# Five staging buffers for the query exponentials, and a new order of all steps

## The chip, the cores and the metric

The kernel runs on one core of a Trainium2 chip. The metric is the device time of one execution in microseconds (us). A core has a matrix engine (TensorE, in the profile PE, with its weight loads as PEld), a vector engine (VectorE, DVE), an activation engine (ScalarE, ACT), a general engine (GpSimd, POOL) and a sync engine (SP) that here only issues transfers. Each engine works off its own list of instructions in order. Transfers (DMAs) are issued by SP and ACT and run on 16 shared DMA engines.

## What is computed

```python
# x: 2048 tokens, D = 448; H = 16 heads of Dh = 28; F = 1792; all bf16
xn = layernorm(x)
q, k, v = split(xn @ wqkv)
phi(t) = concat(softmax(t @ w_phi), softmax(-(t @ w_phi)))     # per head, over 28 features
kv = phi(k)^T @ v ;  z = sum over tokens of phi(k)
a = ((phi(q) @ kv) / (phi(q) . z + 1e-6)) @ wo
h = xn @ w1 + b1 ;  b = (h * tanh(softplus(h))) @ w2           # Mish
out = x + a + b
```

Softmax of the queries needs no sum of its own, since numerator and denominator are divided by each other: for the queries only the exponentials of t and of -t are formed, and the two halves are brought together at the end.

## The kernel before

The 2048 tokens are 16 tiles of 128 (t = 0 to 15), taken as eight pairs (u = 0 to 7). 448 rows of a contraction are three chunks of 128 and one of 64; so that half an array never idles, most products are issued as two streams of 64 rows, one for each tile of a pair, and a product of a pair (a *part step* such as `k3`) is split into two halves, `k31` with 8 and `k32` with 6 matmuls. All of them are recorded on line 438.

Everything is unrolled, and the order of all engines comes from one string, `ORDER`: a list of names of steps. `run_order` calls them one after another; each appends its operations to the lists of its engines, with the resources that it reads and writes, and `Program` derives the waits from them. So the order of the names sets the order on every engine and on SP's and ACT's transfer queues, and it also decides which of the eight banks of the matrix engine's accumulators a step gets (`take1`, `take2`: the least recently used bank or pair that nobody holds).

The names: `l...` loads (`lx3` etc. rows of x, `lkm`, `lvm`, `lkt` the weights of k and v, `lqT` those of q transposed, `l1m`, `l1t` W1, `l2` W2, `lo` Wo; a last letter s is SP, a is ACT). `st` are the statistics of a tile (suffix d on DVE, L467 and L468; suffix a on ACT as a Copy with a sum, a small multiplication and a Square with a sum, L459 to L463); `rs` its reciprocal deviation (suffix p on POOL, a or t on ACT), `xn` the normalised pair (suffix d or p), `xt` its transposition: suffix m by a DMA on SP (L521), a or d by seven matmuls on PE (L509) that ACT or DVE copies out. `wtk` and `wmk`, `wmq` fold w_phi into the weights of k and q (L556, L571). `z` are matmuls on constants before the data arrive (L376). `v`, `k`, `q` are the token products of a pair; when the second half is done, `v` is copied out by ACT or DVE, and `k` and `q` get two exponentials on ACT (exk, L600; exq, L661). `kn` normalises the keys: a sum and a reciprocal on DVE (L608, L610), then a multiplication on POOL (`phik`, L612). `kv` adds up phi(k)^T v over all pairs in one bank (L629), `kvz` masks it on DVE and transposes it by a DMA. `e` is the transposition of a tile of query exponentials to EqT by a DMA on SP (L669). `nd` is numerator and denominator of a tile (PE L703, then DVE), `ot` the transposition of its result by a DMA, `wo` and `G` are the output products (L821 and L805 where whole arrays are used), `f` the first product of the feed-forward layer (`f0` the first 1024 tokens, `f1` the last; 14 chunks of F each, in two halves), followed by Mish on ACT (L680). `sto` and `stt` store a pair or a tile.

Space is shared. The tile `actT` has one row of 2048 columns for each of the 14 chunks of F. Rows 6 to 13 hold the exponentials of the keys (E) until `kv` has read them. The exponentials of the queries (Eq) are staged before their transposition in three buffers: a tile of their own, Eq0 (which early on also holds the transposed weights WT), and rows 4 and 5 of `actT`, in turn by pair number. `p_pads` (`pp`) clears the unused columns of a buffer on POOL. So the Mish of a chunk that lies in such a row waits until the transpositions of that buffer have landed, and an exponential waits for the transpositions of the pair that used its buffer before:

```python
w=[("act", fc, q)] + ([("E", fc - FE, s) for s in range(2)] if fc >= FE else
   [x for i in range(3) if EQ_ROWS[i] == fc for x in (("Eq", i, 0), ("Eq", i, 1), ("Eqp", i))])
```

Of the kernel before, what the change touches and what calls it, by code (L numbers as in the profile page):

```python
# [144 lines left out]


ORDER = """
lpa pp2 lx3s pm z12 st6d pi lkms table st7d pw lx1a lkts lba lvma bd rs3t wtk2a xn3d lx2s lqT2 wtk0d st3d pv wtk1a wmk2a
xt3a wtk3d lqT1 wmk0a wmk1a st2d wmk3a st5d v31d rs1p lqT0 st4d xn1d rs2p lqT3 b1 qd lx6s v32a k31 lx0s wmq1a lx4s pp1
wmq0a xn2p l1ts xt1d st14d st15d wmq2a wmq3a k32 k11 st12d rs7p st9d q11 xt2m st8d k12 st10d xn7d q31 rs4p v11d pp0 q12  # L150
xn4p st11d v12d q21 rs5p st13d q32 q22 xn5p k21 st0d l1m2s l1m0s rs6p xt7m v21d k22 st1d v22a ep e3 rs0p v71a pk xt4m
k71 v72a kn3.1 xn6d k72 xt5m k41 xn0d kn3.0 e2 xt6m xt0m v41d e5 k42 l1m1s v42d e4 q41 v51d q42 e6 e8 v52a kn2.0 k61
v61d k62 kn4.0 k01 k51 kn7.0 kn4.1 k02 v62d q51 k52 q52 kn0.0 e7 q61 e9 v01d q62 e12 kn1.1 kn6.1 e10 f0.11 e11 kn1.0
v02d f0.12 kn0.1 f1.01 f0.21 f1.02 f1.21 kn7.1 f1.31 f1.22 los kn2.1 q71 f1.32 f1.51 kn5.0 f0.22 e13 f1.52 q01 q72 q02
f0.61 l2s kn6.0 kv3 kv1 e15 kv2 kn5.1 kv4 kv6 e14 kv7 kv0 kv5 kvz f0.62 f0.71 f0.91 f1.81 f0.72 e1 f1.82 f0.121 f1.111
f0.122 f0.81 f0.92 f1.112 f0.82 f1.91 f0.131 f1.92 e0 nd2 f0.132 f0.31 f0.101 f0.32 nd0 f0.111 f0.102 f0.112 nd1 f1.71
f1.61 f1.72 f0.51 nd3 f1.62 f0.52 f1.41 f1.11 f0.01 f1.12 f0.41 f1.42 ot0m nd5 f0.42 f0.02 wo01 f1.131 f1.101 ot1m nd6
f1.132 G01 nd4 f1.102 G11 ot2m wob nd7 ot3m G02 wo02 f1.121 nd12 G12 f1.122 wo11 nd11 wo22 G31 wo31 nd10 wo12 G21 nd13
ot5m ot6m wo21 wo32 G62 nd8 G22 wo52 G32 nd9 ot4m wo61 G51 nd15 G61 nd14 wo51 G41 wo62 sto6 sto1 wo41 G52 ot7m g14 sto5
wo7F sto2 G42 wo7H sto0 wo42 g15 stt14 sto3 sto4 stt15  # L160
"""


# [5 lines left out]
def _kernel(es, nc, A_x, A_wqkv, A_w_phi, A_wo, B_w1, B_b1, B_w2, out):  # L169
    def sb(name, shape, dtype):  # L170
        return es.enter_context(nc.sbuf_tensor(name, shape, dtype))
# [30 lines left out]
    actT = sb("actT", [P, FC, S], BF16)  # L202
# [7 lines left out]
    EqT = sb("EqT", [P, NT, 2 * G, P], BF16)  # L210
    Eq0 = sb("Eq0", [P, 4 * TCW], BF16)
# [38 lines left out]
    def bank(b, n=1):  # L250
        return PS[:, b * TCW:(b + n) * TCW]
# [177 lines left out]
    def pair_part(key, part, works, r, then):  # L429
        if part == "1":  # L430
            open_[key] = take2()
        b = open_[key]

        def f(e):
            todo = works(b)
            for par, k, c in halves(part, 3, True):
                o, _, lhs, rhs = todo[par]
                ins = e.matmul(o, lhs(c, k), rhs(c, k), start=part == "1" and c == 0, stop=part == "2" and c == 2)  # L438
# [218 lines left out]

    def q_mm(u, part):
        def then(b):
            for s in range(2):  # L660
                op("ACT", lambda e, s=s: e.activation(  # L661
                    Eq_of(u)[:, :, s, :].rearrange("p i (h n) -> p i h n", n=64)[:, :, :, 0:QP],
                    two(b, D).rearrange("p i (h n) -> p i h n", n=QP), ACT.Exp, scale=1.0 if s == 0 else -1.0),
                   r=[pb(b), pb(b + 1), ("Eqp", u % 3)], w=[("Eq", u % 3, s)], tag=f"exq{u}.{s}")
        pair_part(f"q{u}", part, tok_works(u, Wp[0]), [("xnT", u), ("xnU", u)] + [("Wp", 0, c) for c in range(4)], then)

    def q_turn(t):
        u = t // 2
        dma("SP", lambda e: e.dma_start_transpose(EqT[:, t, :, :], Eq_of(u)[:, t % 2, :, :].rearrange("p s c -> p (s c)")),  # L669
            r=[("Eq", u % 3, 0), ("Eq", u % 3, 1)], w=[("EqT", t)], tag=f"eT{t}")  # L670
# [7 lines left out]
    def ffn1(q, fc, part):  # L678
        def then(b):
            op("ACT", lambda e: e.activation(actT[:, fc, q * 1024:(q + 1) * 1024], bank(b, 2), ACT.Mish,  # L680
                                             bias=b1T[:, fc:fc + 1]),
               r=[("b1T",), pb(b), pb(b + 1)],
               w=[("act", fc, q)] + ([("E", fc - FE, s) for s in range(2)] if fc >= FE else
                                     [x for i in range(3) if EQ_ROWS[i] == fc for x in (("Eq", i, 0), ("Eq", i, 1), ("Eqp", i))]), tag=f"mish{q}_{fc}")
# [181 lines left out]
    def add(name, fn, *args):  # L866
        steps[name] = lambda: fn(*args)
# [120 lines left out]
```

## Time and profile before

| what | value |
|---|---|
| median of three runs | 150.57 us (150.38 to 150.88) |
| the profiled execution's own time | 150.35 us |
| its span in the trace | 148.3 us |
| PE busy | 143.7 us (97%) |
| DVE, ACT, POOL busy | 100.7, 72.0, 44.4 us |
| first product that needs data, end of the last matmul | 5.94, about 145.9 us |

The span runs from the first to the last instruction; the profiled execution's own time is some 2 us longer. The share of a busy engine is an average over stages. In a line of the timeline the first number is the start, the second the time until the last of the grouped instructions ends, and x8 their count; a bracket names an idle time before them and what ended it. In the list of waits the numbers are the total in us, how often, and the longest. A matmul's record is longer than the time it takes from the engine, since matmuls are pipelined; what one costs is read from the distance of the starts.

### The profile page before, as it was taken

The page shows a single profiled execution, that of the slowest core. Times are in us where ns is not written, and L with a number is a line of the kernel's source. Part 1 is how long each engine was busy: PE and PEld are TensorE (multiplying, and loading weights), DVE is VectorE, ACT ScalarE, POOL GpSimd, SP SyncE. Part 2 cuts the span into 40 slices and gives each one's busy share as a digit, 9 for nine tenths or more (in the row PEclk, how much of TensorE's full clock was granted, in tenths as well). Part 3 has the DMA queues.
Part 4 walks back from the last instruction along what each step waited for, and adds up shares of the span by engine and source line. Part 5 has one row for each costly group of instructions (what it writes and reads, how often), then busy time and mean ns, then how long its engine had stood idle before and what let it go on. Part 6 is the DMA issues. An engine that isn't in the chain of part 4 may idle for free.

```text
span 148.3 us, 3988 instructions
## 1 busy us (share of the span) xinstructions
PE 143.7 (97%) x1731; PEld 75.9 (51%) x1731; DVE 100.7 (68%) x225; ACT 72.0 (49%) x83; POOL 44.4 (30%) x65
## 2 busy tenths in 40 slices
PE   7799999999999999999999999999999999999993
PEld 2456456556555475444454445555555555554452
DVE  0888889897999803003998278896789859983042
ACT  3589889978996899578566653202000000000000
POOL 5428489899899990000000000000000000000000
PEclk9999999999999999999999999999999999999999
DMA  5999998999939989960003300031003300306513
GB/s 123 301 190 346 182 275 130 163 205 256 139 67 174 242 242 267 210 113 0 0 4 62 62 4 0 21 73 34 4 2 66 62 0 4 62 4 186 186 52 134
DMA packets 39997, 17.24 MB, mean 116 GB/s; under 512 B 33964, under 2 KB 39212, under 8 KB 39980
## 3 DMA queue, kind: packets, MB, share of 16 engines
q1 hardware_dynamic: 38800, 16.29, 52.5%
q10 hardware_dynamic: 1180, 0.70, 1.9%
q8 instruction: 13, 0.21, 0.6%
q14 instruction: 4, 0.03, 0.1%
HBM read 7.02 MB, written 1.84 MB: 60 GB/s over the span
## 4 chain that ended last, share of the span: by engine, by line
PE 89%; DMA 6%; DVE 2%; issue 0%; ACT 0%; SPq 0%
PE PS L438 47%; PE PS L843 31%; PE PS L805 3%; DMA Wkv<-in_A_wqkv_dram 3%; DMA xnT<-xn 3%; PE PS L703 2%; PE PS L629 2%; PE PS L571 1%; PE PS L821 1%; DVE stats L467 1%; PE PS L556 1%; PE PS L509 1%; DVE xnT L516 0%; ACT Eq L514 0%; DVE x_all L770 0%
## 5 line engine op out<-in xcount | busy, mean ns | idle before, releaser
L438 PE MATMUL PS<-xnT,W 64*128 64x512 bf16 x392 | 44.8, 376 | 0.0
L680 ACT ACTIVATE actT<-PS,b1T 128x1024 bf16<-128x1024 f32 x28 | 30.1, 1112 | 24.3 <-PE PS L438 24.3
L843 PE MATMUL PS<-W,actT 64*128 64x448 bf16 x392 | 39.3, 349 | 0.0
L438 PEld LDWEIGHTS PS<-xnT,W 64*128 64x128 bf16 x392 | 18.8, 94 | 20.8 <-ACT actT L680 0.5
L843 PEld LDWEIGHTS PS<-W,actT 64*128 64x128 bf16 x392 | 18.1, 94 | 18.1 <-issue 0.3
L612 POOL TENSOR_TENSOR actT<-actT,rSk 128x896 bf16<-128x896 bf16 x16 | 26.6, 1702 | 0.7 <-DVE rSk L610 0.6
L770 DVE TENSOR_TENSOR x_all<-PS,x_all 128x448 bf16<-128x448 f32 (+1 forms) x16 | 9.2, 616 | 11.3 <-PE PS L821 5.6
L718 DVE COPY Sq<-PS 128x16 f32<-128x16 f32 x32 | 4.1, 169 | 18.6 <-PE PS L703 18.5
L608 DVE TENSOR_REDUCE Sk<-actT 128x32 f32<-128x896 bf16 x16 | 16.7, 1043 | 0.0
L600 ACT ACTIVATE actT<-PS 128x896 bf16<-128x896 f32 x16 | 13.8, 950 | 1.0 <-PE PS L438 0.9
L438 PE MATMUL PS<-Wkv,xnT 64*128 64x448 bf16 x112 | 13.2, 349 | 0.0
L438 PE MATMUL PS<-Wpq,xnT 64*128 64x448 bf16 x112 | 12.5, 349 | 0.4 <-DMA xnT<-xn 0.4
L467 DVE BATCH_NORM_STATS2 stats<-x_all 128x6 f32<-128x448 bf16 x16 | 9.7, 608 | 4.1 <-DMA x_all<-in_A_x_dram 4.1
L438 PE MATMUL PS<-Wpk,xnT 64*128 64x448 bf16 x112 | 12.5, 349 | 0.0
L726 DVE TENSOR_TENSOR v_all<-v_all 128x464 f32<-128x464 f32 x16 | 10.3, 642 | 0.6
L722 DVE TENSOR_TENSOR v_all<-PS,Sq 128x464 f32<-128x464 f32 x16 | 10.3, 642 | 0.5
L729 DVE TENSOR_TENSOR xn<-v_all,rden 128x448 bf16<-128x448 f32 x16 | 10.0, 625 | 0.6
L724 DVE TENSOR_TENSOR v_all<-PS,Sq 128x464 f32<-128x464 f32 x16 | 10.1, 631 | 0.0
L661 ACT ACTIVATE actT<-PS 128x896 bf16<-128x896 f32 x10 | 8.6, 921 | 1.1 <-PE PS L438 1.1
L438 PEld LDWEIGHTS PS<-Wpq,xnT 64*128 64x128 bf16 x112 | 5.9, 94 | 5.4 <-issue 0.8
L438 PEld LDWEIGHTS PS<-Wpk,xnT 64*128 64x128 bf16 x112 | 6.0, 94 | 4.4
L438 PEld LDWEIGHTS PS<-Wkv,xnT 64*128 64x128 bf16 x112 | 6.0, 94 | 4.3
(82 smaller groups left out, 126.4 us busy)
## 6 DMA issues: line engine op xcount, KB each, us to landing
W<-in_B_w_dram SPq DMA_DIRECT2D x1, 1568.0 KB, 10.1
out_dram<-x_all SPq DMA_DIRECT2D x7, 224.0 KB, 2.1
W<-in_B_w_dram SPq DMA_DIRECT2D x3, 448.0 KB, 4.1
x_all<-in_A_x_dram SPq DMA_DIRECT2D x2, 448.0 KB, 4.9
x_all<-in_A_x_dram SPq DMA_DIRECT2D x3, 224.0 KB, 3.8
Wo<-in_A_wo_dram SPq DMA_DIRECT2D x2, 336.0 KB, 4.1
W<-in_B_w_dram SPq DMA_DIRECT2D x2, 224.0 KB, 6.4
Wkv<-in_A_wqkv_dram SPq DMA_DIRECT2D x1, 336.0 KB, 4.5
```

The costliest lines, as they stand in the source:

```text
L438: ins = e.matmul(o, lhs(c, k), rhs(c, k), start=part == "1" and c == 0, stop=part == "2" and c == 2)
L467: op("DVE", lambda e: e.bn_stats(stats[:, t, :], x_all[:, t, :]), r=[("x", t)], w=[("st", t)], tag=f"bn{t}")
L600: op("ACT", lambda e, s=s: e.activation(E_of(u)[:, s, :, :], two(b, D), ACT.Exp, scale=1.0 if s == 0 else -1.0), r=[pb(b), pb(b + 1)], w=[ ...
L608: op("DVE", lambda e: e.tensor_reduce(Sk[u][:, s, :], Eh(), AX.X, ALU.add), r=[("E", u, s)], w=[("Sk", u, s)], tag=f"Sk{u}.{s}")
L612: op("POOL", lambda e: e.tensor_tensor(Eh(), Eh(), ap_on(rSk[u][:, s, 0:1], [[1, 2 * H], [0, DH]]), ALU.mult), r=[("E", u, s), ("rSk", u, ...
L680: op("ACT", lambda e: e.activation(actT[:, fc, q * 1024:(q + 1) * 1024], bank(b, 2), ACT.Mish, bias=b1T[:, fc:fc + 1]), r=[("b1T",), pb(b) ...
L722: op("DVE", lambda e: e.tensor_tensor(tv(t1[i]), num(0), sx(1), ALU.mult), r=[pb(b), pb(b + 1), ("Sq", i, 1)], w=[("t1", i)], tag=f"ta{t}")
L724: op("DVE", lambda e: e.tensor_tensor(tv(t2), num(1), sx(0), ALU.mult), r=[pb(b), pb(b + 1), ("Sq", i, 0)], w=[("t2",)], tag=f"tb{t}")
L726: op("DVE", lambda e: e.tensor_tensor(t1[i], t1[i], t2, ALU.add), r=[("t1", i), ("t2",)], w=[("t1", i)], tag=f"tc{t}")
L729: op("DVE", lambda e: e.tensor_tensor(o_sb[(t // 2) % 2][:, t % 2, :].rearrange("p (h d) -> p h d", d=DH), t1[i][:, :, 0:DH], ap_on(rden[i ...
L770: op("DVE", lambda e: e.tensor_tensor(x_all[:, t, 0:n], bank(b)[:, 0:n], x_all[:, t, 0:n], ALU.add), r=[pb(b), ("x", t)], w=[("out", t)], ...
L843: ins = e.matmul(bank(places[par][0])[:, 0:D], l, r, start=fresh[par], stop=places[par][2] and i >= len(todo) - 2)
```

## The change

`EQ_ROWS` gets rows 3 and 2 of `actT` as a fourth and fifth buffer, and a table says which pair uses which: u0, u1 and u6 Eq0; u3 and u7 row 4; u2 row 5; u4 row 3; u5 row 2. Two more pad steps clear them. `ORDER` is replaced. The first loads stand in the same order on each queue (on ACT the table load comes behind them in the list). Some steps change their engine: st6 from DVE to ACT; rs7, rs0 and rs2 from POOL to ACT (rs2 as one for each tile), rs3, on ACT before too, for both tiles at once; xn2, xn4 and xn5 from POOL to DVE, xn7 and xn0 from DVE to POOL; xt2 from a DMA to PE and DVE; the copy of wmq0 to DVE; v1 is copied by ACT and v2 by DVE, v7 by DVE, v6 and v4 by ACT, v5 by DVE; W2 is loaded from ACT's queue. z12 becomes z10.

```diff
 ORDER = """
-lpa pp2 lx3s pm z12 st6d pi lkms table st7d pw lx1a lkts lba lvma bd rs3t wtk2a xn3d lx2s lqT2 wtk0d st3d pv wtk1a wmk2a
-xt3a wtk3d lqT1 wmk0a wmk1a st2d wmk3a st5d v31d rs1p lqT0 st4d xn1d rs2p lqT3 b1 qd lx6s v32a k31 lx0s wmq1a lx4s pp1
-wmq0a xn2p l1ts xt1d st14d st15d wmq2a wmq3a k32 k11 st12d rs7p st9d q11 xt2m st8d k12 st10d xn7d q31 rs4p v11d pp0 q12
-xn4p st11d v12d q21 rs5p st13d q32 q22 xn5p k21 st0d l1m2s l1m0s rs6p xt7m v21d k22 st1d v22a ep e3 rs0p v71a pk xt4m
...
+lpa lx1a lba lvma lx3s lkms lkts lx2s lqT2 lqT1 lqT0 lqT3 lx6s lx0s lx4s table pw pp0 z10 st7d pm st3d st6a l1m1s pi
+st2d bd b1 rs3a xn3d wtk2a wtk1a l1m2s wtk0d wmk2a rs1p xt3a pp2 xn1d wmk1a wtk3d wmk0a xt1d st4d wmk3a st5d pp4 v31a
+v11d rs2t xn2d st15d v32a v12a k11 qd st14d wmq1a wmq2a xt2d rs7a xn7p wmq3a wmq0d k12 st12d st13d k31 st8d st9d k21 pp1
+rs6p xt7m xn6d rs4p st0d xn4d k32 st11d pk q21 k22 q22 v21a pp3 q11 v22d xt6m ep q31 st10d rs5p xt4m q12 st1d q32 xn5d
+rs0a l1m0s v71d pv xn0p k71 v72d xt5m k72 k61 e3 kn3.1 v61a k62 k41 v41a e2 kn2.1 v62a k42 q41 xt0m v42a q42 l1ts q51
+v51d kn2.0 kn4.0 q52 e8 e9 kn4.1 kn3.0 q61 v52d q62 k51 e4 e5 kn1.0 kn1.1 kn6.0 k01 k52 kn5.1 f0.11 v01d k02 v02d e12
+f1.01 f0.12 f1.31 f1.51 e13 f1.32 f1.02 e10 kn0.0 kn0.1 f1.52 e7 e11 f0.31 q71 f0.21 e6 f0.32 kn7.1 q01 f0.22 f0.131 q02
+q72 kv4 kv1 kn6.1 e0 kv3 kv2 kv0 kn5.0 kv6 kv5 kn7.0 kv7 kvz f0.91 e14 f0.132 f1.101 e1 los f1.81 e15 f1.102 f1.82 f1.61
+f0.92 wob f1.62 f0.121 nd0 l2a f1.11 f1.21 f1.12 nd1 f0.122 f1.22 f0.51 f0.41 ot0m f0.52 nd3 f1.71 f0.42 f1.72 f0.01
...
+wo42 G32 wo7F g14 wo7H G52 stt14 sto4 sto1 sto3 g15 sto5 sto6 stt15
 """
...
-    EQ_ROWS = (None, 4, 5)
+    EQ_ROWS = (None, 4, 5, 3, 2)
+    NEQ = len(EQ_ROWS)
+    EQ_BUF = (0, 0, 2, 1, 3, 4, 0, 1)
+
+    def Eq_buf(i):
+        if EQ_ROWS[i] is None:
+            return Eq0[:, :].rearrange("p (i s c) -> p i s c", i=2, s=2)
+        return actT[:, EQ_ROWS[i], :].rearrange("p (i s c) -> p i s c", i=2, s=2)
 
     def Eq_of(u):
-        if u % 3 == 0:
-            return Eq0[:, :].rearrange("p (i s c) -> p i s c", i=2, s=2)
-        return actT[:, EQ_ROWS[u % 3], :].rearrange("p (i s c) -> p i s c", i=2, s=2)
+        return Eq_buf(EQ_BUF[u])
...
-                   r=[pb(b), pb(b + 1), ("Eqp", u % 3)], w=[("Eq", u % 3, s)], tag=f"exq{u}.{s}")
+                   r=[pb(b), pb(b + 1), ("Eqp", EQ_BUF[u])], w=[("Eq", EQ_BUF[u], s)], tag=f"exq{u}.{s}")
...
-            r=[("Eq", u % 3, 0), ("Eq", u % 3, 1)], w=[("EqT", t)], tag=f"eT{t}")
+            r=[("Eq", EQ_BUF[u], 0), ("Eq", EQ_BUF[u], 1)], w=[("EqT", t)], tag=f"eT{t}")
...
-                                     [x for i in range(3) if EQ_ROWS[i] == fc for x in (("Eq", i, 0), ("Eq", i, 1), ("Eqp", i))]), tag=f"mish{q}_{fc}")
+                                     [x for i in range(NEQ) if EQ_ROWS[i] == fc for x in (("Eq", i, 0), ("Eq", i, 1), ("Eqp", i))]), tag=f"mish{q}_{fc}")
...
-    for i in range(3):
+    for i in range(NEQ):
         add(f"pp{i}", p_pads, (i,))
```

More of the change, by code (lines that the diff above doesn't have):

```diff
@@ L147 @@
 ORDER = """
-lpa pp2 lx3s pm z12 st6d pi lkms table st7d pw lx1a lkts lba lvma bd rs3t wtk2a xn3d lx2s lqT2 wtk0d st3d pv wtk1a wmk2a
-xt3a wtk3d lqT1 wmk0a wmk1a st2d wmk3a st5d v31d rs1p lqT0 st4d xn1d rs2p lqT3 b1 qd lx6s v32a k31 lx0s wmq1a lx4s pp1
-wmq0a xn2p l1ts xt1d st14d st15d wmq2a wmq3a k32 k11 st12d rs7p st9d q11 xt2m st8d k12 st10d xn7d q31 rs4p v11d pp0 q12
-xn4p st11d v12d q21 rs5p st13d q32 q22 xn5p k21 st0d l1m2s l1m0s rs6p xt7m v21d k22 st1d v22a ep e3 rs0p v71a pk xt4m
-k71 v72a kn3.1 xn6d k72 xt5m k41 xn0d kn3.0 e2 xt6m xt0m v41d e5 k42 l1m1s v42d e4 q41 v51d q42 e6 e8 v52a kn2.0 k61
@@ L153 @@
[L153 to L157, printed above, removed]
@@ L158 @@
-f1.132 G01 nd4 f1.102 G11 ot2m wob nd7 ot3m G02 wo02 f1.121 nd12 G12 f1.122 wo11 nd11 wo22 G31 wo31 nd10 wo12 G21 nd13
-ot5m ot6m wo21 wo32 G62 nd8 G22 wo52 G32 nd9 ot4m wo61 G51 nd15 G61 nd14 wo51 G41 wo62 sto6 sto1 wo41 G52 ot7m g14 sto5
-wo7F sto2 G42 wo7H sto0 wo42 g15 stt14 sto3 sto4 stt15
+lpa lx1a lba lvma lx3s lkms lkts lx2s lqT2 lqT1 lqT0 lqT3 lx6s lx0s lx4s table pw pp0 z10 st7d pm st3d st6a l1m1s pi
+st2d bd b1 rs3a xn3d wtk2a wtk1a l1m2s wtk0d wmk2a rs1p xt3a pp2 xn1d wmk1a wtk3d wmk0a xt1d st4d wmk3a st5d pp4 v31a
@@ new lines @@
+q72 kv4 kv1 kn6.1 e0 kv3 kv2 kv0 kn5.0 kv6 kv5 kn7.0 kv7 kvz f0.91 e14 f0.132 f1.101 e1 los f1.81 e15 f1.102 f1.82 f1.61
+f0.92 wob f1.62 f0.121 nd0 l2a f1.11 f1.21 f1.12 nd1 f0.122 f1.22 f0.51 f0.41 ot0m f0.52 nd3 f1.71 f0.42 f1.72 f0.01
+f1.131 nd2 f0.02 f0.61 f1.132 nd4 f0.62 f0.111 f0.81 f0.112 nd5 f0.82 f1.121 f0.101 ot2m nd12 ot1m f0.71 f1.122 f0.72
+f0.102 f1.41 f1.111 f1.42 f1.112 nd6 G12 wo21 nd7 G11 nd13 wo11 ot3m f1.91 wo12 G02 nd10 G21 ot6m f1.92 nd11 G01 nd9
+wo22 G22 wo61 nd8 G61 ot5m sto2 nd14 G41 G62 ot4m wo62 nd15 G42 wo51 wo31 wo41 wo01 ot7m G51 wo02 sto0 wo32 wo52 G31
@@ L345, in p_pads @@
         for i in which:
-            op("POOL", lambda e, i=i: e.memset(Eq_of(i).rearrange("p i s (h n) -> p (i s h) n", n=64)[:, :, QP:64], 0.0),
+            op("POOL", lambda e, i=i: e.memset(Eq_buf(i).rearrange("p i s (h n) -> p (i s h) n", n=64)[:, :, QP:64], 0.0),
                w=[("Eqp", i)] + ([("WT", c) for c in range(4)] if i == 0 else []), tag=f"pp{i}")
```

## The prediction

> **What bounds the kernel now.** I read the page first, then a table of stretches, then the chain of waits, then the timelines of single engines.
>
> ```profile
> span 148.3 us, 3988 instructions
> ...
> PE 143.7 (97%) x1731; PEld 75.9 (51%) x1731; DVE 100.7 (68%) x225; ACT 72.0 (49%) x83; POOL 44.4 (30%) x65
> ```
> ```profile
> core 0: us, PE busy (x) PEld busy (x) DVE busy (x) ACT busy (x) POOL busy (x), PEclk, DMA share, GB/s
> ...
> 9.06:18.64 9.58, 9.19 (x104) 4.87 (x103) 8.35 (x28) 8.15 (x14) 5.92 (x13) 1.00 0.99 238
> 18.64:53.12 34.48, 34.48 (x351) 19.23 (x352) 30.44 (x57) 30.49 (x34) 32.56 (x34) 1.00 1.01 178
> ...
> 98.50:145.38 46.88, 46.88 (x577) 24.25 (x574) 31.76 (x71) 1.11 (x1) 0.00 (x0) 1.00 0.23 60
> ```
> PE is busy 97% of the span and never stops after 18.64 until the last product. The time is therefore PE's list of work, plus the start before PE's stream closes up, plus the last store. The profiled run took 150.35 us around its span of 148.3; the median of the three runs is 150.57, so a difference found in the trace is added to 150.57.
>
> Which waits could the five buffers remove? A wait for a transposed Eq would name a DMA of EqT. The list of waits has only these four that name a DMA:
> ```profile
> DVE stats L467 <- DMA x_all<-in_A_x_dram: 4.1, 2, 3.6
> ...
> POOL Wbd L544 <- DMA Wraw<-in_A_w_phi_dram: 1.1, 1, 1.1
> ...
> PE PS L556 <- DMA Wkv<-in_A_wqkv_dram: 0.4, 1, 0.4
> ...
> PE PS L438 <- DMA xnT<-xn: 0.4, 1, 0.4
> ...
> PEld PS L438 <- ACT actT L680: 0.5, 2, 0.4
> ```
> None is on Eq: the third buffer is not what anything waits for. The buffers only permit a new order, and the new order is what must be priced.
>
> **The change on PE.** PE's products stay the same in number. Two warm matmuls go (z12 to z10, before any real work), and seven transposes of xt2 come in, because that pair now goes through PE and not through a DMA. Rates, from the chain and the PE timeline:
> ```profile
> 11.56 0.50 PE PS L571 x8
> 12.06 0.41 PE PS L509 x7
> ...
> 53.19 3.27 PE PS L629 x128
> ...
> 68.87 3.02 PE PS L438 x28
> ```
> ```profile
> 9.06 0.93 PE L438 MATMUL PS<-Wkv,xnT 64*128 64x448 bf16 x8
> ...
> 32.64 2.83 PE L438 MATMUL PS<-Wpk,xnT 64*128 64x448 bf16 x28
> 35.29 0.75 PE L438 MATMUL PS<-Wkv,xnT 64*128 64x448 bf16 x6
> ```
> A 448-wide product of half the rows costs (35.29 − 32.64)/28 = 0.0946, a 512-wide one 3.02/28 = 0.108, the four products of a wmq 0.25, seven transposes 0.41, one kv 3.27/8 = 0.41.
>
> From the first v31 to the first kv both orders hold 24 token steps (24 × 14 × 0.0946 = 31.8), 92 products of f (9.9; counting the steps gives 92 in both orders) and four wmq (1.0). Before, xt1 and b1 lie in it too (0.5), 43.2 in all, and they take 53.12 − 9.06 = 44.06. So 0.9 is lost: 0.7 before 18.64 (9.58 less 78 × 0.0946 and 1.5), 0.2 after. In the new order xt2 lies in it (0.4), and xt1 and b1 come before v31: 43.1.
>
> **The start.** Everything turns on when v31 may begin, S. Before it was 9.06 (the first row of PE's timeline above).
> ```profile
> 3.64 0.63 DVE L467 BATCH_NORM_STATS2 stats<-x_all 128x6 f32<-128x448 bf16 x1 [3.64 <-DMA x_all<-in_A_x_dram]
> ...
> 5.17 1.23 DVE L501 TENSOR_SCALAR xn<-x_all,mv,rstd 128x448 bf16<-128x448 bf16 x3
> ...
> 8.28 0.42 DVE L516 COPY Eq<-PS 112x512 bf16<-112x512 bf16 x1 [0.50 <-PE PS L556]
> ...
> 9.37 0.59 DVE L467 BATCH_NORM_STATS2 stats<-x_all 128x6 f32<-128x448 bf16 x1
> ...
> 10.10 0.60 DVE L467 BATCH_NORM_STATS2 stats<-x_all 128x6 f32<-128x448 bf16 x1
> ...
> 10.83 0.86 DVE L501 TENSOR_SCALAR xn<-x_all,mv,rstd 128x448 bf16<-128x448 bf16 x3
> ```
> ```profile
> 1.27 1.28 ACT L315 ACT_TABLE_LOAD   x1 [1.27 <-PEq L973]
> 1.30 0.48 ACTq L270 DMA_DIRECT2D x_all<-in_A_x_dram  x1
> ...
> 9.85 0.71 POOL L476 TENSOR_TENSOR rstd<-lnv,mhalf 128x2 f32<-128x2 f32 x1
> ```
> ```profile
> x_all<-in_A_x_dram ACTq DMA_DIRECT2D x1, 224.0 KB, 4.1
> ```
> DVE now takes st3 and st2 ahead of xn3. Their rows of x are issued at 1.30 and land 4.1 later, at 5.4. Two statistics at 10.10 − 9.37 = 0.73 end at 6.9; b1's small copy 0.1; xn3 then ends at 7.8, where it ended at 6.4 before (5.17 + 1.23). PE's xt3 waits for it until 7.9. On DVE there follow the copy of wtk0 (0.42, to 8.2) and xn1 (0.86, to 9.0; its rstd is ready at 8.1, statistics at 6.9, then 0.71 on POOL and a smaller operation ahead of it), then the copy of wtk3 (to 9.4). PE meanwhile does xt3, wmk1, wtk3, wmk0, xt1 and, after the copy of wtk3, wmk3: 9.4 + 0.1 + 0.36 gives S = 9.85. Between 9.75 (no gaps) and 10.1 (each hand-over 0.1 longer); I take 9.85. st6 on ACT is not late: no row shows Copy or Square with a sum, the nearest (ACT's passes over twice as much, 0.95 each, below) bounds two of them by 1.9, and three small operations add some 0.7; from 3.64 that is 6.2 at the most, and DVE reaches xn3 at 7.0: 0.
>
> After S: xnT1 is there at 10.2, needed at 10.6; xn2 at 13.1, needed at 13.75; xn7 on POOL ends near 17.5 (rs7 at 15.6 on ACT, then under 2 us), and xt7's transpose lands 3.7 later at the median of the transposes of EqT quoted below, at 21.2, or at their slowest 6.1 at 23.6; v71 needs it at 23.1. So PE should run through the place of its 0.40 wait. I keep the 0.2 of loss that stood after 18.64: kv begins at 9.85 + 43.1 + 0.2 = 53.15, against 53.12. The bounds are 52.85 (S = 9.75, no loss) and 54.1 (S = 10.1, the old loss of 0.9). The 0.8 by which S comes later buys a closed stream: **sum 0.0**.
>
> **Cover that this uses.** POOL's sixteen phik gate kv:
> ```profile
> 28.00 9.98 POOL L612 TENSOR_TENSOR actT<-actT,rSk 128x896 bf16<-128x896 bf16 x6
> 38.62 16.61 POOL L612 TENSOR_TENSOR actT<-actT,rSk 128x896 bf16<-128x896 bf16 x10 [0.64 <-DVE rSk L610]
> ```
> That is 1.66 each, 26.6. DVE has more ahead of kn3.1 now (xn2, xn4, xn5 come to it, xn7 and xn0 leave), from 15.6 on eight statistics at 0.73, three xn at 0.86 and, by estimate, 3.2 for two copies of v and small ones, 11.6 with nothing between; allowing 1.5 for waits POOL begins near 28.7 and ends near 55.3; the last kv starts at 53.15 + 7 × 0.41 = 56.0. Cost 0, up to +0.5 if DVE slips. ACT does as many passes as before, the same three table changes too (q0 and q7 still lie among the f). l1t moves behind xt0 on SP, to about 32 or 33; before it landed 6.4 after its issue, behind the loads of x, so it is there by 38.4 to 39.4 at the latest, and f0.11 starts at 38.5 (S, 20 and a half token steps, 1.4): 0, at most +0.9.
> ```profile
> W<-in_B_w_dram SPq DMA_DIRECT2D x2, 224.0 KB, 6.4
> ```
> The load of W2 goes from SP to ACT's queue, 20 us ahead of its use: 0. The pads pp3 and pp4 are two more small memsets at places where POOL waits for statistics: 0. After kv the list of work is the same; DVE, which empties the banks of nd, is busy 31.8 of the last 46.9 us, so a few nd's closer together wait a little and others less: 0, from −0.5 (the two waits for ACT go) to +0.4. At the end stt14, sto4, sto1 and sto3 stand on SP behind the finish of wo7H.
> ```profile
> L861 SPq DMA_DIRECT2D out_dram<-x_all x8: 332/394/458, 133.5 to 144.2; - x8
> ```
> Four issues of 0.39 are covered by G52 (28 × 0.0946 = 2.6) and g15 behind it: 0 to +0.3.
>
> **The rivals.** *Late transposes (slower).* Row 2 of the activations is now a buffer, so the Mish of f0.2 must wait for e11, and kv4 takes the bank that this Mish empties. e11 is the ninth transpose in a row on SP.
> ```profile
> 31.45 1.24 SPq L669 DMA_TRANSPOSE EqT<-actT  x1
> ...
> 38.47 1.31 SPq L669 DMA_TRANSPOSE EqT<-actT  x1
> ```
> ```profile
> L680 ACT ACTIVATE actT<-PS,b1T 128x1024 bf16<-128x1024 f32 x28 | 30.1, 1112 | 24.3 <-PE PS L438 24.3
> ...
> L600 ACT ACTIVATE actT<-PS 128x896 bf16<-128x896 f32 x16 | 13.8, 950 | 1.0 <-PE PS L438 0.9
> ```
> The answer for the tile EqT adds the times to landing:
> ```profile
> DMA to landing us min/median/max: 3.2/3.7/6.1
> ```
> The run of nine begins when exq4 is done: q42 ends 16 token steps, wmq and xt2 after S, at 32.4, and ACT then has some 2.4 us ahead (exq4 and the copy of v4, three passes of 13.8/16). That is 34.8. At the issue's own 1.31 e11 is issued at 45.3 and lands at 49; at the pace of these four, (38.47 − 31.45)/4 = 1.75, it is issued at 48.8 and lands at 52.5, at the slowest landing at 54.9. It decides from 52.0 on: f0.22 ends 2.0 ahead of kv4 (eight products of f and twelve of q), near 51.1, its Mish takes 1.1, and kv4 wants the bank at 53.1. Price from 0.5 (52.5) to 2.9, likeliest near 1: 151.1 to 153.5. For it: nine in a row is longer than any run shown. Against it: those four had a 448 KB load ahead of them. Chance 0.2.
> The Trainium skill, DMA: Bandwidth & Descriptors (Latency and other measured facts), gives a DMA transpose 261 GB/s; a tile of 128 by 1024 two-byte numbers would then take an estimated 1.0 us, SP's issue would be the limit, and this rival would fall. The rows at 1.75 do not agree with it; which holds here no row of before decides.
>
> *A late start (slower).* If Square is not in the table that ACT holds, two loads of 1.28 put st6's end at 8.1, xn3 1.15 later, and S with it: 151.7. Or the shorter warm-up leaves PE slow:
> ```profile
> 0.85 4.65 PE L376 MATMUL PS<-const-bfloat16-1.0 128*128 128x512 bf16 x12 [0.85 <-PEq L973]
> ...
> 4.90 0.60 PE L376 MATMUL PS<-const-bfloat16-1.0 128*128 128x512 bf16 x2
> 5.12 0.38 PE L376 MATMUL PS<-const-bfloat16-1.0 128*128 128x512 bf16 x1
> ```
> Of the twelve, ten start within 4.05 us (0.85 to 4.90), the last two 0.22 apart: the rate doubled near 4.8. Ten of them end near 5.0, just past it. If the doubling comes later, the 2 us of PE work between 7.9 and S take 4: 152.6 or more. Chance of both together 0.12.
> The Trainium skill, TensorE: Matmul & The Clock Gate (Part 1), has the clock released after a busy window of about 3.4 us whose phase is free; the doubling some 4 us after the first matmul agrees, and by that rule two matmuls fewer are missed in some executions only.
>
> *All gaps close (faster).* If S is 9.75, and neither the 0.2 nor the two waits for ACT (0.5) recur, 0.8 goes: 149.8. Against it: the new order has the same four pairs of banks. Chance of −0.45 or better 0.16.
>
> **How the numbers follow.** No change within the closed ledger, 150.6, own range 150.1 to 151.0: 0.52. Late transposes 0.2, late start 0.12, faster 0.16. 0.3% is 0.45 us, about what the three runs differ by among themselves (150.38 to 150.88). Of the two slow cases nearly all lies above 0.3%: slower 0.32; same 0.52; faster 0.16. The range from 149.8 to 152.2 leaves out the slow matmuls and the far end of the late transposes, under 0.1.
>
> **What would show it.** Right: v31 at 9.8 to 10.1, no PE wait for xnT near 18, kv at 53.1, no wait of ACT L680 for EqT. Wrong: v31 after 10.5; an extra table load on ACT before 6; a PE wait just ahead of the first kv, with ACT waiting for a transpose; a longer stretch between the last kv and g15.

## The result, and the profile after

The changed kernel took 152.44 us (median of six runs, 151.87 to 155.3), the kernel before 150.58 on the same chip (150.32 to 150.88). The ratio is 1.0116, with a 95% interval of 1.0086 to 1.0147: slower by 1.2%. The run of 155.3 us, at a granted clock of 0.978, is left out of this ratio and not of the median, and so it is with such runs below. The forecast was 150.6, no change; the upper end of its range was 152.2.

The page of the changed kernel and its table of stretches. Lines of the code have moved by five (L438 is now L443, L680 is L685, L669 is L674, L629 is L634, L509 is L514, L556 is L561).

```profile
span 150.2 us, 4003 instructions
...
PE 145.2 (97%) x1736; PEld 76.0 (51%) x1736; DVE 101.9 (68%) x227; ACT 73.9 (49%) x93; POOL 40.4 (27%) x58
...
W<-in_B_w_dram ACTq DMA_DIRECT2D x1, 1568.0 KB, 10.8
```
```profile
10.57:53.80 43.23, 43.23 (x455) 21.75 (x453) 39.42 (x81) 38.26 (x53) 32.70 (x36) 1.00 0.79 169
53.80:57.20 3.40, 3.40 (x132) 3.27 (x132) 0.00 (x0) 3.39 (x5) 2.85 (x3) 1.00 0.02 5
57.20:72.00 14.80, 14.80 (x180) 6.95 (x182) 7.55 (x19) 11.28 (x12) 0.24 (x1) 1.00 0.93 217
72.00:78.00 6.00, 5.19 (x64) 2.16 (x60) 3.87 (x9) 3.27 (x4) 0.00 (x0) 1.00 0.63 130
```
PE is busy 97% of the span in both kernels, so the page alone tells nothing apart. The stretches do. PE is busy without a break from 10.57 to 72, then there is a hole of 0.8 us between 72 and 78, which the kernel before does not have. The waits name it, in a row that the kernel before did not have at all, the one for a transposed Eq:

```profile
ACT actT L685 <- DMA EqT<-actT: 3.3, 2, 2.6
...
PE PS L679 <- DMA b_rows<-in_B_b_dram: 0.9, 1, 0.9
...
PE PS L708 <- ACT actT L685: 0.8, 1, 0.8
```
The timeline, with PE, ACT and the two DMA queues, in order of time:

```profile
0.85 4.43 PE L381 MATMUL PS<-const-bfloat16-1.0 128*128 128x512 bf16 x10 [0.85 <-PEq L978]
6.18 0.17 PE L679 MATMUL PS<-ident,b_rows 14*128 14x14 bf16 x1 [0.91 <-DMA b_rows<-in_B_b_dram]
6.28 1.53 PE L561 MATMUL PS<-ident,Wkv 128*112 128x128 bf16 x12
...
8.00 0.95 PE L514 MATMUL PS<-ident,xn 128*128 128x128 bf16 x7
...
10.57 2.82 PE L443 MATMUL PS<-Wkv,xnT 64*128 64x448 bf16 x28
...
35.90 1.93 SPq L674 DMA_TRANSPOSE EqT<-actT  x1
...
52.34 1.11 ACT L685 ACTIVATE actT<-PS,b1T 128x1024 bf16<-128x1024 f32 x1 [0.74 <-DMA EqT<-actT]
...
53.78 3.42 PE L634 MATMUL PS<-actT,v_all 128*60 128x112 bf16 x128
...
64.05 0.42 ACTq L310 DMA_DIRECT2D W<-in_B_w_dram  x1
...
65.07 2.63 SPq L674 DMA_TRANSPOSE EqT<-actT  x1
...
75.10 3.37 ACT L685 ACTIVATE actT<-PS,b1T 128x1024 bf16<-128x1024 f32 x3 [2.59 <-DMA EqT<-actT]
76.27 0.39 PE L708 MATMUL PS<-KVZ,EqT 56*128 56x60 bf16 x16 [0.81 <-ACT actT L685]
```
The chain of waits passes through two transposes, e11 at 47.51 and e15 at 65.07 (start, then the time to the landing), and the tile EqT shows how far e15 is out of the ordinary:

```profile
47.51 4.77 DMA EqT<-actT
...
65.07 9.96 DMA EqT<-actT
```
```profile
DMA to landing us min/median/max: 3.0/3.3/10.0
```
e15 is issued 1.0 us behind W2's load and lands at 75.03; W2's 1568 KB land at 64.05 + 10.8 = 74.9. The median of the sixteen is 3.3 us, this one takes 10.0 and lands as W2 is done. e15 reads row 4 of the activations, so the Mish of f0.4, which writes that row, waits 2.59 us, and PE waits 0.81 for ACT.

So there are two losses. kv begins at 53.78 instead of 53.12 (+0.66). From kv to the end of the span it takes 150.2 − 53.78 = 96.4, against 148.3 − 53.12 = 95.2 before (+1.2). The sum is the difference of the spans, 1.9.

### The profile page after: what moved, and what is told of

It reads as the page before. It is cut to its first block, busy times and chain, and to the rows that moved or that the text cites. A ratio compares the mean times of both kernels' runs of the same rounds, so it can differ in the third digit from the quotient of the medians.

```text
span 150.2 us, 4003 instructions
## 1 busy us (share of the span) xinstructions
PE 145.2 (97%) x1736; PEld 76.0 (51%) x1736; DVE 101.9 (68%) x227; ACT 73.9 (49%) x93; POOL 40.4 (27%) x58
## 4 chain that ended last, share of the span: by engine, by line
PE 71%; DMA 13%; ACT 6%; SPq 6%; issue 1%; ACTq 1%; DVE 0%
PE PS L848 31%; PE PS L443 30%; DMA EqT<-actT 10%; SPq L674 5%; PE PS L810 3%; DMA b_rows<-in_B_b_dram 3%; PE PS L708 2%; ACT actT L685 2%; SPq L317 1%; PE PS L576 1%; PE PS L561 1%; ACT Eq L666 1%; ACT actT L666 1%; PE PS L514 1%; PE PS L826 1%
## 5 line engine op out<-in xcount | busy, mean ns | idle before, releaser
L443 PE MATMUL PS<-xnT,W 64*128 64x512 bf16 x392 | 44.7, 376 | 0.0
L685 ACT ACTIVATE actT<-PS,b1T 128x1024 bf16<-128x1024 f32 x28 | 29.9, 1112 | 26.7 <-PE PS L443 23.1
L443 PEld LDWEIGHTS PS<-xnT,W 64*128 64x128 bf16 x392 | 18.2, 94 | 21.5 <-ACT actT L685 0.9
L848 PEld LDWEIGHTS PS<-W,actT 64*128 64x128 bf16 x392 | 18.6, 94 | 16.6
L443 PE MATMUL PS<-Wkv,xnT 64*128 64x448 bf16 x112 | 12.6, 349 | 0.0
L443 PE MATMUL PS<-Wpq,xnT 64*128 64x448 bf16 x112 | 12.4, 349 | 0.0
L472 DVE BATCH_NORM_STATS2 stats<-x_all 128x6 f32<-128x448 bf16 x15 | 9.1, 610 | 4.6 <-DMA x_all<-in_A_x_dram 4.6
L443 PE MATMUL PS<-Wpk,xnT 64*128 64x448 bf16 x112 | 12.1, 349 | 0.0
L729 DVE TENSOR_TENSOR v_all<-PS,Sq 128x464 f32<-128x464 f32 x16 | 10.1, 630 | 0.0
L443 PEld LDWEIGHTS PS<-Wpq,xnT 64*128 64x128 bf16 x112 | 5.4, 94 | 5.3
L708 PEld LDWEIGHTS PS<-KVZ,EqT 56*128 56x128 bf16 x256 | 5.7, 93 | 4.5 <-ACT actT L685 1.3
L443 PEld LDWEIGHTS PS<-Wkv,xnT 64*128 64x128 bf16 x112 | 5.4, 94 | 5.1
## 6 DMA issues: line engine op xcount, KB each, us to landing
W<-in_B_w_dram ACTq DMA_DIRECT2D x1, 1568.0 KB, 10.8
```

The costliest lines, as they stand in the source:

```text
L729: op("DVE", lambda e: e.tensor_tensor(tv(t2), num(1), sx(0), ALU.mult), r=[pb(b), pb(b + 1), ("Sq", i, 0)], w=[("t2",)], tag=f"tb{t}")
L848: ins = e.matmul(bank(places[par][0])[:, 0:D], l, r, start=fresh[par], stop=places[par][2] and i >= len(todo) - 2)
```

## The experiments

All times below are medians; each ratio is to the kernel before, run on the same chip. Two numbers of each trace carry the account: when kv begins (PE's first L634, or L629 in the kernel before), and the span left behind it. Without the stall near 75 us that second number is 95.2 to 95.6 in every trace.

| kernel | time, us | ratio, 95% interval | v31 begins | kv begins | span − kv |
|---|---|---|---|---|---|
| before | 150.58 | 1 | 9.06 | 53.1 | 95.2 |
| changed | 152.44 | 1.0116 (1.0086 to 1.0147) | 10.57 | 53.8 | 96.4 |
| e1 z12 | 152.22 | 1.0126 (1.0099 to 1.0153) | 10.22 | 53.4 | 97.0 |
| e2 W2 late | 151.25 | 1.0053 (1.0036 to 1.007) | 10.95 | 54.2 | 95.3 |
| e3 both | 150.43 | 1.0013 (0.9989 to 1.0036) | 10.38 | 53.6 | 95.3 |
| e4 before with z10 | 150.30 | 1.0 (0.9975 to 1.0025) | 9.18 | 54.6 | 95.3 |
| e5 Wo behind e15 | 150.90 | 1.0024 (1.0 to 1.0048) | – | – | – |
| e6 f0.4 late | 151.38 | 1.0059 (1.0036 to 1.0082) | 10.97 | 54.2 | 95.3 |
| e7 three buffers | 157.98 | 1.0502 (1.0469 to 1.0535) | 10.35 | 60.3 | 95.6 |
| e8 b1, e11 | 150.67 | 1.0021 (0.9997 to 1.0046) | 10.03 | 53.4 | 95.3 |
| e9 old start | 151.92 | 1.0095 (1.007 to 1.0119) | 9.41 | 54.6 | 95.3 |
| e10 b1 late, z10 | 151.20 | 1.0041 (1.0016 to 1.0066) | 10.30 | 53.6 | 95.3 |
| e11 old start, mended | 151.30 | 1.0054 (1.0033 to 1.0074) | 9.74 | 54.4 | 95.3 |

### W2 against the transpose: e2, e5, e6

**e2**, the load of W2 moved behind nd3, 7.7 us later (71.77 instead of 64.05):

```diff
-... nd0 l2a f1.11 f1.21 f1.12 nd1 f0.122 f1.22 f0.51 f0.41 ot0m f0.52 nd3 f1.71 ...
+... nd0 f1.11 f1.21 f1.12 nd1 f0.122 f1.22 f0.51 f0.41 ot0m f0.52 nd3 l2a f1.71 ...
```


> The new order with the load of W2 moved on ACT's queue from behind nd0 to behind nd3, some 8 us later, so that e15 lands before it starts. Theory (the 1568 KB of W2 share the DMA engines with e15, which therefore lands 10.0 us after its issue; the Mish of f0.4, whose row e15 reads, waits for it, and PE for the bank): e15 lands within 5 us, ACT's wait of 2.6 us for EqT is gone, the stretch from the first kv to g15 shrinks by 1.0 to 1.2 us, time near 151.3. Rival (e15 is late because four loads of Wo stand ahead of it in SP's own queue): e15 still lands 8 us or more after its issue and the time stays at 152.4.

**e5**, W2 left where the change put it, the loads of Wo (which stood ahead of e15 on SP) moved behind e15, so that e15 is issued ahead of W2:

```diff
-... f1.101 e1 los f1.81 e15 f1.102 ...
+... f1.101 e1 f1.81 e15 los f1.102 ...
```


> The changed kernel with the eight loads of Wo moved behind the transpose e15 in the list; W2's load stays where the change put it, and ten warm-up matmuls stay. Theory (W2's 1568 KB meet the transpose in time): e15 is issued near 62.7 us instead of 65.07, ahead of W2's issue at 64.05, lands in 5 us or less, the wait of Mish f0.4 for it (2.59 us) goes, and the time is about 151.3 us. Rival (it is not the meeting, any later load delays it as much, or Wo's loads now take W2's part): the transpose lands at 75 us again or Mish waits for another, 152.4 us.

**e6**, both loads left, the halves of Mish f0.4 and f0.6 exchanged, so that the late transpose is awaited by nobody:

```diff
-... f0.51 f0.41 ot0m f0.52 nd3 f1.71 f0.42 ... nd2 f0.02 f0.61 f1.132 nd4 f0.62 ...
+... f0.51 f0.61 ot0m f0.52 nd3 f1.71 f0.62 ... nd2 f0.02 f0.41 f1.132 nd4 f0.42 ...
```


> The changed kernel with the places of the halves of Mish f0.4 and f0.6 exchanged in the list, so that the Mish of the buffer that e15 reads is issued some 10 us later; W2's load and ten warm-up matmuls stay. Theory (W2's load harms only through the one Mish that waits for e15): e15 still lands some 10 us after its issue, but no Mish waits for it and PE has no wait of over 0.3 us ahead of nd2; about 151.3 us. Rival (W2's transfer slows more than this transpose): the time stays at 152.4 us though that wait is gone.

All three take the stall away, in different ways. e2 gives 151.25 and e6 151.38, where the theory said 151.3; e5 gives 150.90. In e2 the slowest transpose lands in 5.0 us. In e6 it is as late as ever, and it no longer matters. The tile EqT of e2, and then of e6:

```profile
DMA to landing us min/median/max: 3.0/3.4/5.0
```
```profile
DMA to landing us min/median/max: 3.0/3.3/10.7
```
The timeline of e6 at the place of the stall, where ACT's and PE's brackets for EqT are gone:

```profile
73.53 2.12 ACT L685 ACTIVATE actT<-PS,b1T 128x1024 bf16<-128x1024 f32 x2 [0.62 <-PE PS L443]
...
75.69 0.39 PE L708 MATMUL PS<-KVZ,EqT 56*128 56x60 bf16 x16
```
So W2's load costs only through the one Mish that waits for e15. (In e5's profiled execution TensorE was granted 0.67 of its clock and it took 218.48 us, so its trace is not compared with the others; within it, e15 is issued 4.7 us ahead of W2, no transpose takes more than 5.4 us to land, and no wait of ACT names EqT.)

### The warm-up: e1, e3, e4, e10

**e1** is the changed kernel with `z12` for `z10`; **e3** is e1 with e2's late W2; **e4** is the kernel before with `z10` for `z12`.

> The new order with twelve warm matmuls instead of ten, nothing else. In the changed kernel's trace the twelve transposes of wtk run 1.46 us (0.85 before) and the first xt 0.75 (0.39 before), with matmuls of 314 ns where they took 219. Theory (two warm matmuls too few leave PE at half rate in the start): these return to 0.85 and 0.39, v31 starts near 10.0 instead of 10.6, and the time falls by 0.5 to 0.7 us against the changed kernel, to about 151.7. Rival (v31 is late because the rows of b1 land at 6.05 and because DVE's list is longer): v31 stays at 10.5, the time at 152.4.

> Both edits in the new order: twelve warm matmuls, and W2 behind nd3. Theory (two separate causes): the gains add, 1.5 to 1.9 us, time 150.5 to 150.9, no different from the kernel before by 0.3%. Rival (one hides behind the other, or the earlier start is lost again in front of kv, where the Mish of f0.2 waits for e11): the sum is below 1.2 us, time over 151.2, and ACT shows a wait for EqT of over 0.7 us near 52.

> The kernel before with ten warm matmuls instead of twelve, nothing else. Theory (the warm-up decides): the twelve wtk transposes take longer than 0.85 us, v31 starts 0.3 to 0.7 later than 9.06, time 150.9 to 151.2. Rival (PE is warm by either, and the new order's sparser start lost it): no change, 150.6, transposes at 0.85.

In e1 PE reaches the full rate within the first twelve transposes. Its PE timeline, and its ACT and PE near 75 us:

```profile
6.21 1.15 PE L561 MATMUL PS<-ident,Wkv 128*112 128x128 bf16 x12
...
8.01 0.56 PE L514 MATMUL PS<-ident,xn 128*128 128x128 bf16 x7
...
10.22 1.50 PE L443 MATMUL PS<-Wkv,xnT 64*128 64x448 bf16 x14
...
75.29 3.37 ACT L685 ACTIVATE actT<-PS,b1T 128x1024 bf16<-128x1024 f32 x3 [3.14 <-DMA EqT<-actT]
76.45 0.40 PE L708 MATMUL PS<-KVZ,EqT 56*128 56x60 bf16 x16 [1.36 <-ACT actT L685]
```
Twelve transposes take 1.15 us instead of 1.53 (0.88 in e3, where all are at the full rate), seven 0.56 instead of 0.95, and v31 begins 0.35 earlier. Yet the time hardly moved. The row at 75 says why: Mish f0.4 starts at 75.29, not earlier than the 75.10 of the changed kernel, because it waits for e15, which was issued 0.38 earlier (64.69 against 65.07) and yet landed no earlier (75.21 against 75.03); why it took longer is not shown. PE's wait there grew from 0.81 to 1.36. What PE gained at the start it lost at the stall. The expectation of 0.5 to 0.7 failed for that reason. With the stall gone the same edit is worth 151.25 − 150.43 = 0.8 (e2 to e3), and W2's place is worth 1.2 with ten warm-up matmuls and 1.8 with twelve. e3 is level with the kernel before.

e4 shows that ten matmuls are enough for the old order: no change in the median. (Its profiled execution, 151.85 us, is the longest of its twelve: kv is late there by a wait of 1.2 us for xnT near 27 us, not by the start.) The next run asks whether the changed order is slow at the start because of PE's idle time ahead of b1. **e10** is e2 with b1 moved behind k1, so that PE does not wait for b_rows:

```diff
-st2d bd b1 rs3a xn3d ...
+st2d bd rs3a xn3d ...
-v11d rs2t xn2d st15d v32a v12a k11 qd ...
+v11d rs2t xn2d st15d v32a v12a k11 b1 qd ...
```


> The changed kernel with W2's load behind nd3 (151.25 us), ten warm-up matmuls as it has, and the step b1 moved behind k1. Theory (PE's slow matmuls at the start come from its idle stretch between warm-up and b1, 1.4 us in that version): the weight transposes start at 5.95 us, the idle stretch is 1.0 us or less, no transposes of a block take over 0.6 us for seven, v31 starts near 10.1 us instead of 10.95, 150.5 us. Rival (ten warm-up matmuls are too few for the later start whatever stands behind them): slow matmuls up to 10 us again, v31 at 10.6 us, 150.9 to 151.2 us.

The profiled execution is as the theory said, the runs are not: 151.20 is level with e2's 151.25. The PE timeline of e2, then of e10:

```profile
0.85 3.86 PE L381 MATMUL PS<-const-bfloat16-1.0 128*128 128x512 bf16 x10 [0.85 <-PEq L978]
...
6.24 0.88 PE L561 MATMUL PS<-ident,Wkv 128*112 128x128 bf16 x12
...
7.85 0.93 PE L514 MATMUL PS<-ident,xn 128*128 128x128 bf16 x7
```
```profile
0.85 4.42 PE L381 MATMUL PS<-const-bfloat16-1.0 128*128 128x512 bf16 x10 [0.85 <-PEq L978]
6.00 0.85 PE L561 MATMUL PS<-ident,Wkv 128*112 128x128 bf16 x12 [0.73 <-DMA Wkv<-in_A_wqkv_dram]
...
8.09 0.56 PE L514 MATMUL PS<-ident,xn 128*128 128x128 bf16 x7 [0.62 <-DVE xn L506]
```
With ten warm-up matmuls the start came out in three ways in these traces: slow from the first real work (changed kernel, twelve transposes in 1.53), fast and then slow again from 7.4 us (e2 and e6, twelve in 0.88 and then seven in 0.93), fast throughout (e10). e10's twelve runs lie between 150.43 and 153.29. With twelve it was fast from the first transposes on in e3, e7, e8, e9 and e11 (0.85 to 0.91), and in e1 from their middle on.

One kernel does more than one of these. In e2's trace the second slow stretch shows as a granted clock of half; its page, each digit a slice of 3.7 us:

```profile
PEclk9959999999999999999999999999999999999999
```
A stretch of 3.4 us at half the clock (7.41 to 10.82 us) makes a mean of 0.989 over the span, and that mean is on record for each execution. It is below 0.99 in seven of e2's twelve (151.17 to 151.62 us) and above in the other five (150.43 to 151.01); in e10 it is below in five (151.34 and more) and above in seven. So the two traces above show two kinds of execution, not what moving b1 does, and e10 does not show that b1's wait matters. Over the kernels with the new order and five buffers the mean is below 0.99 in 25 of 53 executions with ten warm-up matmuls (the one at 0.67 not counted) and in 3 of 48 with twelve: the two matmuls make this slow stretch rare. What decides it in a single execution stays open.

The Trainium skill, TensorE: Matmul & The Clock Gate (Part 1), says that the clock follows activity in a window of about 3.4 us that runs freely, so that the point of change depends on where the window falls at the start. The same ten matmuls took 4.43, 3.86 and 4.42 us here, and e2's stretch at half the clock lasted 3.4 us, which agrees. What brings the slow rate back is not shown: in e2 a gap of 1.44 us and a thin stretch behind it stood ahead of it, but e4 has a gap of 1.48 us (until 6.04 us) and stays at the full rate, with a mean of at least 0.999 in all its twelve executions.

### The buffers: e7

**e7** is e3 with the three buffers of before; the transposes e4 to e7 move to where their buffer is needed, and Mish f1.5 and f1.2 exchange places:

```diff
-    EQ_ROWS = (None, 4, 5, 3, 2)
+    EQ_ROWS = (None, 4, 5)
-    EQ_BUF = (0, 0, 2, 1, 3, 4, 0, 1)
+    EQ_BUF = (0, 1, 2, 0, 1, 2, 0, 1)
```


> The version with twelve warm-up matmuls and W2's load behind nd3 (150.43 us), with three buffers for the query exponentials instead of five: the buffers are those of before, the transposes e4 to e7 move to where their buffer is needed, and Mish f1.5 and f1.2 exchange places. Theory (no wait is on these buffers in the kernel before, so two more of them buy only a freedom of order): within 0.3% of 150.4 us. Rival (the exponentials wait for transposes with three buffers): ACT waits for them ahead of kv and the time is 150.9 us or more.

My theory fell, by far: 157.98 against 150.43. Its waits:

```profile
PEld PS L443 <- ACT actT L666: 4.3, 1, 4.3
ACT actT L666 <- DMA EqT<-actT: 4.3, 1, 4.3
...
ACT Eq L666 <- DMA EqT<-Eq: 3.0, 1, 3.0
```
The new order runs the blocks of q closer together, and with three buffers the exponentials of two of them wait 4.3 and 3.0 us for transposes; kv begins at 60.3, 6.7 us later than in e3. Not all of that is waiting. From 30 us to 46.8 us PE is idle for 4.1 us; most of the rest is its clock, which fell to half during PE's wait and stayed there from 39.9 to 46.8 us (the page, each digit a slice of 3.9 us):

```profile
PEclk9999999999659999999999999999999999999999
```
In that stretch PE is busy for 4.8 us; at a granted 0.50 this is an estimated 2.4 us lost. That no wait in the kernel before names Eq was true and said nothing of this order: in it the lack of two buffers costs some 7 us. (Another order for three buffers need not wait so long; the kernel before is one that has no such wait.)

### A version below both: e8, e9, e11

**e8** is e3 with b1 behind k1 and e11 ahead of e7. **e9** gives e8 the start of the kernel before: st6 and st7 both on VectorE and first, xn3 ahead of st3 and st2, and v31, v32, k31 ahead of xt1.

```diff
-... z12 st7d pm st3d st6a l1m1s pi st2d bd rs3a xn3d wtk2a ... xt1d st4d wmk3a st5d pp4 v31a
+... z12 st6d st7d pm l1m1s pi bd rs3t wtk2a xn3d ... st4d wmk3a xn1d st5d pp4 v31a
-v11d rs2t xn2d st15d v32a v12a k11 b1 qd st14d wmq1a wmq2a xt2d ...
+v32a k31 b1 qd wmq1a wmq2a xt1d rs2t xn2d v11d v12a k11 st15d st14d xt2d ...
```
**e11** is e9 with `v32a xt1d k31` and with b1 and qd behind k11 again.

> The version with twelve warm-up matmuls and W2's load behind nd3 (150.43 us), with the step b1, which waits for b_rows until 6.37 us, moved behind k1, and with the transpose e11 ahead of e7. Theory: the twelve weight transposes start at 5.95 us instead of 6.47, v31 starts near 9.9 us instead of 10.38, ACT's wait for e11 near 52 us (1.0 us) goes, and the time is 149.9 us, below both kernels. Rival (VectorE's chain of statistics and normalised rows sets the start of v31, not PE's row of transposes): v31 stays at 10.3 us and the time at 150.4 us.

> The version with twelve warm-up matmuls, W2's load behind nd3, b1 behind the first blocks and e11 ahead of e7 (150.67 us), with the start in the order of the kernel before: the statistics of rows' tiles 6 and 7 both on VectorE and first, xn3 ahead of the statistics of tiles 3 and 2, and v31, v32, k31 ahead of the transposes of xn1. Theory (ACT's statistics of tile 6 and the two behind it on VectorE, not PE, set the start of v31): xn3 starts near 5.2 us instead of 6.90, v31 at 9.1 us instead of 10.03, and with the stretch from v31 to kv at 43.2 to 43.4 us the last products of keys and values start near 52.4 us; 149.7 us, below both kernels. Rival (the gaps that the new order closed behind v31 come back when PE starts earlier): v31 at 9.1 us but that stretch at 44 us, and 150.5 us.

> The version with the start of the kernel before (151.92 us; v31 at 9.41 us, but kv at 54.62 us, 45.2 us behind it, where the version with v31 at 10.03 us has kv 43.3 us behind), with the transposes of xn1 moved ahead of k31 and the loads' copies of q's weights (qd) and b1 back behind k11, so that k31's eight matmuls cover the copy of xnT that v11 waits for (1.1 us of idle there now). Theory (the early start lost its gain in the order of five steps behind it alone): v31 at 9.4 us again, no wait of PE for xnT near 12 us, the stretch to kv at 43.2 to 43.5 us, kv near 52.8 us, 150.0 us, below the kernel before by 0.3%. Rival (VectorE has no room for the earlier start: statistics, rows and copies come as late as before): PE waits of 0.5 us or more move to the next blocks, kv at 53.3 us or later, 150.5 us or more.

The PE timelines of e8, of e9 and of e11:

```profile
5.92 0.91 PE L561 MATMUL PS<-ident,Wkv 128*112 128x128 bf16 x12
...
10.03 2.82 PE L443 MATMUL PS<-Wkv,xnT 64*128 64x448 bf16 x28
```
```profile
9.41 1.74 PE L443 MATMUL PS<-Wkv,xnT 64*128 64x448 bf16 x14
...
13.63 1.74 PE L443 MATMUL PS<-Wkv,xnT 64*128 64x448 bf16 x14 [0.72 <-DVE xnT L521]
```
```profile
6.28 0.85 PE L561 MATMUL PS<-ident,Wkv 128*112 128x128 bf16 x12 [0.83 <-DMA Wkv<-in_A_wqkv_dram]
...
9.74 1.74 PE L443 MATMUL PS<-Wkv,xnT 64*128 64x448 bf16 x14
```
In e8 the start came forward as the theory said (v31 at 10.03, and ACT's wait for e11 is gone), but kv by 0.2 only, and the time not at all: level with e3 and with the kernel before. In e9 and e11 v31 begins earlier still, and kv later: it is 45.2 and 44.7 us behind v31, against 43.3 in e8. Of that, 0.4 is xt1, which now lies behind v31 and not ahead of it. e9 also has a wait of 0.72 us for VectorE's copy of xnT; in e11, where PE's idle time is 0.2 us in all, the other 1.0 is spread over waits of its weight loads of 0.5 us at most. The times are those of the rivals or worse; their reason, that in this order VectorE and ACT have no room to feed PE earlier, fits e9's wait but is argued and not shown. None of these versions is measurably faster than the kernel before.

## Why the prediction was wrong

**The step that failed: "The load of W2 goes from SP to ACT's queue, 20 us ahead of its use: 0."** I asked only whether W2 would be in time for its own reader. It was. What it did was to hold back e15, issued 1.0 us behind it on the other queue. The row for the load before, 10.1 us, would have given the length of the shadow, the time in which the load can hold up others; the two orders side by side would have shown that e15 stands in it, and that f0.4, the Mish of its row, stands close behind. Its cost is 1.2 us (changed kernel to e2), 1.8 when PE starts in time (e1 to e3). The kernel before has the same shadow, with W2 on SP itself. The row on its page, and SP's timeline:

```profile
W<-in_B_w_dram SPq DMA_DIRECT2D x1, 1568.0 KB, 10.1
```
```profile
50.16 0.65 SPq L305 DMA_DIRECT2D W<-in_B_w_dram  x1
...
55.01 4.75 SPq L669 DMA_TRANSPOSE EqT<-actT  x2
```
The next transposes are issued 4.9 us behind the load, the slowest one of that kernel takes 6.1 to land, and nothing waits for it.

The Trainium skill, DMA: Bandwidth & Descriptors (Queues, rings and completion order), says that the SP and ACT queues use the same 16 DMA engines, and that each engine turns from one queue to the next after a packet. By that rule moving a load to the other queue takes it out of the order of issue and not out of the way. That e15 was held up by a load on the other queue agrees. That it landed no sooner than the load itself (75.03 against 74.9), though it is a sixth of its size, is more than the rule says, and no run here shows the reason.

**The rival *Late transposes* named the right kind of wait at the wrong place.** Its transpose, e11, was issued as the ninth at 47.51 and landed 4.77 us later, at 52.3; I had it at 52.5 and its threshold at 52.0. ACT did wait 0.74 for it (the row at 52.34), but no wait of PE shows ahead of kv, since kv was itself 0.66 later than forecast. Taking that wait away (e8, which also moves b1) brought nothing that can be measured. The pace of the nine was (47.51 − 35.9)/8 = 1.45 us, between the 1.31 and the 1.75 that I had as bounds.

**The start: S was 9.85 in the forecast and 10.57 in the trace.** The chain on VectorE was right to 0.2: in e8, warm and without the wait for b_rows, S is 10.03. The rest is b1's wait, 0.91 us until 6.18, which I had not priced at all (I counted its copy on VectorE, not the landing that PE stands still for; without it v31 comes 0.35 earlier, e3 to e8), and the slow rate. (The two, 0.35 each, are more than the 0.54 between 10.57 and 10.03; b1's start alone moves by 0.2 between traces, 6.15 in e2 and 6.37 in e3.) The slow rate is the second half of the rival *A late start*, right in kind; I gave it 2 us, it cost 0.35 at the start (e1 against the changed kernel) and 0.8 in the medians (e2 to e3). Square needed no extra table load, so the other half of that rival did not occur. Of the signs named, two of the wrong ones came: v31 after 10.5, and a longer stretch from kv to g15; of the right ones, that ACT would not wait for EqT did not hold.

**What held.** The stream after v31 closed as forecast: 43.2 us from v31 to kv (forecast 43.3), and the 0.40 wait for xnT is gone. POOL's phik cost nothing. The end cost nothing: without W2's stall the span behind kv is 95.3, against 95.2 before. That the buffers only permit an order held as far as the kernel before goes; e7 shows that this order needs them.

So the ledger was 0.0 and should have been +1.9: +0.66 at kv, +1.2 behind it.

## What to carry to other kernels

When a load is moved to another queue, price not only its own reader but every transfer issued during its flight, and who waits for those: here a transpose issued 1.0 us behind a large load landed only with it. A gain ahead of a wait for a DMA can be lost there, as in e1, where the transfer was issued earlier and landed no earlier; so take the last wait away first, and measure the other edits after it. And "no wait names this resource" holds for the order that was profiled, not for the next one. A trace is one execution: where a kernel has two kinds, as e2 has, compare the lists of runs before reading an edit out of two traces.

## What the runs showed of the hardware that was not expected

- A transpose of 256 KB that lands in 3.3 us at the median took 10.0 (10.7 in e6) when 1568 KB were issued 1.0 us ahead of it on the other queue. Its issue on SP took 2.63 us instead of 1.34, but 2.15 in e2 too, where that load was not in flight.
- The rate of PE at the start differs between executions of nearly the same code: twelve transposes took 1.53 us in one trace and 0.88 in another, with the same ten matmuls ahead. The granted clock shows it in e2 (half for 3.4 us) and not in the changed kernel, whose table of stretches has 1.00 while seven transposes take 0.95 us instead of 0.56; the durations of the matmuls show it in both.
- Statistics of a tile on ACT, which no row of before showed, took (5.75 + 0.19) − 4.24 = 1.7 us, with an operation of its own behind each pass to read the sum. ACT's timeline of e8:

```profile
4.24 0.58 ACT L464 ACTIVATE junk<-x_all 128x448 bf16<-128x448 bf16 x1
...
4.72 0.19 ACT L464 ACTIVATION_READ_ACCUMULATOR junk<-x_all 128x1 f32 x1
...
5.17 0.67 ACT L468 ACTIVATE junk<-x_all,rmean 128x448 bf16<-128x448 bf16 x1
5.75 0.19 ACT L468 ACTIVATION_READ_ACCUMULATOR junk<-x_all,rmean 128x1 f32 x1
```
